# Attention and two feed-forward products on one core: v in six loads by SyncE, k asked for in mid-batch, six moves by GpSimd's queue

## The chip, the cores and the metric

The kernel runs on 1 core of one Trainium2 chip. The metric is the device time of one execution in microseconds (us); each kernel is timed in several runs and the median counts. One more execution of each kernel was recorded by the hardware profiler. All durations and waits below come from such a recording.

In the rows PE is TensorE (matmul), PEld its weight loads, DVE VectorE, ACT ScalarE, POOL GpSimd, SP SyncE. SP computes nothing here: it asks for transfers. A "q" behind an engine's name is its instruction queue: "SPq L281" is SP issuing the transfer of line 281.

## The reference

Attention over 4 batches of 12 heads (448 tokens, 64 wide) whose scores are mixed over the heads ahead of the softmax and again behind it; then two feed-forward products over the 1792 tokens.

```
scores = scale * np.matmul(q, k.transpose(0, 1, 3, 2))
scores = np.einsum('bhij,hg->bgij', scores, w_pre)
attn = softmax(scores)                       # exp(scores - max) / (sum + 1e-9)
attn = np.einsum('bhij,hg->bgij', attn, w_post)
x = np.matmul(attn, v)                       # -> 1792 x 768
x = ((x @ w1) * (x @ w2)) @ w3 @ w_out       # widths 1024, 1024, 768
out = leaky(x @ w_in) @ w_out2               # max(0.01 h, h), width 2048
```

## The kernel before

**Stages.** The attention fills the first 372 us of the span; what follows are the feed-forward products, in which TensorE is busy 99% of the time or more. The change touches the attention alone. The order of all instructions behind it is the same in both kernels, engine by engine.

**Tiling of the attention.** A batch's 448 rows of scores are cut into four chunks (120, 120, 120 and 88 rows). The 12 heads go in 6 pairs `p`. For each chunk and pair, `qk` (L242) makes the raw scores in PSUM, ACT or DVE copies them to a tile `s` (L254, L256), and `move` (L281) carries each head's rows by DMA from SBUF to SBUF into one of three row tiles `sr`, where rows of all heads stand in the partitions together, so that `premix` (L315) can mix the heads as one matmul. A chunk is 12 moves (the last head takes two pieces, so 13 transfers), 210 KB each for a full chunk. Then, for each group of two blocks of rows: `premix` (PE, pm), `tops` (DVE, mx, L325), `softmax` (ACT, e, L332), `weigh` (mostly POOL, e, L348: the division by the sum), `postmix` (PE, po, L369, and DVE transposes to `ap`, L384), and `av` (PE, px, L401), the product with v.

**The loop.** Groups are numbered through all batches, 23 a batch (6, 6, 6 and 5 a chunk). The main loop takes `k` = 0, 2, 4, ...; one turn is called a step, and `do(k // 2, ...)` counts them. A step runs `qk` for the groups ten ahead (LEAD), `tops` and `softmax` of groups k and k+1, `av` for two pairs of a finished chunk, `postmix` of groups k-2 and k-1, and `premix` of groups k+2 and k+3. The first `premix` of a chunk needs all its 13 moves landed. Chunk 2 of the first batch starts with group 12, mixed at the end of step k = 10.

**What sets the order.** The attention is written out by hand (`manual_schedule`): each engine takes its instructions in the order of the program text. `at(step, job, ...)` puts loads of q and k and their splits (`upper` on ACT, `lower` on DVE) at steps counted back from the step that needs them (`need`). Nearly all transfers are issued by SP, in order, on one queue. The program gives its SP and ACT transfers eight semaphores in turn, so that a transfer is issued only when the one that holds its semaphore from eight places earlier has landed.

**v and k.** `vs` holds v of one batch (six pairs, 256 KB each). Batch 0's v is one load of 1536 KB on ACT's queue at the end of step 0 (L551); those of batches 1 to 3 are three loads of 512 KB by SP, each behind the `av` of two pairs in the last chunk of the batch before. k of a batch is three loads of 448 KB (two pairs each), asked for four steps ahead of need. For batches 2 and 3 these are the very steps in which v is loaded too; call this stretch the seam between two batches. The row tiles of the chunks go on being filled through it.

**The start.** The ten groups' worth of `qk` that run ahead of the loop cover the first chunk and part of the second. The first chunk's moves are cut in two halves (105 KB each): first halves of even heads on ACT's queue, of odd heads on SP's; second halves of odd heads on SP's, and of the six even heads on ACT's queue, three at k = 7 and three at k = 9 of that first loop (L465).

Of the kernel before, what the change touches and what calls it, by code (L numbers as in the profile page):

```python
# [22 lines left out]
def attention_moe_kernel(ctx: ExitStack, tc, qt, kt, vt, w_pre, w_post, w1, w2, w3t, w_out, w_in2, w_out2, out):  # L23
# [7 lines left out]
    nc = tc.nc  # L31
    B, _, NPAIR, S = kt.shape
# [85 lines left out]
    def attention(seam):  # L118
        with ExitStack() as es, ExitStack() as left:
# [60 lines left out]
            NC = len(chunks)  # L180
            HN, PLAIN, KROOM, QROOM = NPAIR // 2, NC, 9, 7
            vs = late.tile([P, NPAIR, NJ, 2, D], F32, tag="vs", name="vs", bufs=1)
# [22 lines left out]
            def q_load(b, c, a):  # L205
                load("q", (b, c, a), qt[b, c][:, a * HN:(a + 1) * HN, :])
# [9 lines left out]
                lo_dve(lo, raws[key][1], hi)  # L216
                give(key[0], [raws.pop(key)])

            def v_load(b, p0, p1, queue=nc.sync):
                queue.dma_start(out=vs[:, p0:p1], in_=vt[b, p0:p1].rearrange("n p j e d -> p n j e d"))  # L220

            def qk(b, c, p, early=False):

# [214 lines left out]
            def slot(k):  # L438

                b, c, t, nt = where[k]  # L440
                return [(b, c, p) for p in range(NPAIR) if min(p, nt - 1) == t]
# [10 lines left out]
            for k in range(LEAD):  # L452
                for x in slot(k):
                    qk(*x, early=True)
                if k == 1:
                    turn(4)
                if k == 5:
                    constants()
                    for args in second[1::2]:
                        move(*args, nc.sync, 1)  # L460
                        if not queued and args[-1] > 4:
                            queued.append([q_load(*order[2], a) for a in range(2)])
                if k in (7, 9):
                    for args in second[(k - 7) * 3:][:6:2]:
                        move(*args, nc.scalar, 1)  # L465
            turn(6)

            jobs = {}
# [1 line left out]
            def at(step, job, *args):  # L470

                jobs.setdefault((max(step, 0), job), []).append(args)
# [17 lines left out]
            for i in range(3, len(order)):  # L490
                for a in range(2):
                    need = step_of(i, a * HN)
# [3 lines left out]
            for b in range(1, B):  # L496
                for g in range(HN):
                    need = step_of(b * NC, 2 * g)
                    at(need - 4, k_load, b, g)
                    parted("k", (b, g), need)  # L500

            premix(0)
# [3 lines left out]
            for k in range(0, NG + 2, 2):  # L506
                if k:
                    flush(queue=nc.scalar if k + LEAD > NG else nc.sync)
                while later:
                    stores.append(later.pop(0))  # L510
                now = [g for g in (k, k + 1) if g < NG]
                done = [g for g in (k - 2, k - 1) if g >= 0]
                fresh = [n for g in now for n in groups[g]]
                old = [n for g in done for n in groups[g]]
                before = ets.pop(k - 2, None)
                ahead = [x for g in now if g + LEAD < NG for x in slot(g + LEAD)]
                for x in ahead:
                    qk(*x)
                for job in (k_load, q_load):
                    do(k // 2, job)  # L520
                if fresh:
                    tops(fresh)
                    sm, ets[k] = softmax(fresh)
                evict()
                do(k // 2, lower)
                drain = not ahead
                for _ in range(min(4 if len(todo) > NPAIR else 2, len(todo)) if now else len(todo)):
                    b, c, p = todo.pop(0)
                    av(b, c, p)
                    if c == NC - 1 and b < B - 1 and p % 2:  # L530
                        v_load(b + 1, p - 1, p + 1)
                turns = []
                if drain:
                    if old:
                        turns = postmix(old, before, now=False)
                        turn_out(turns.pop(0))
                    if k > LAST:
                        next(seam, None)
                    if now:
                        weigh(fresh, sm, ets[k], True)  # L540
                    while turns:
                        turn_out(turns.pop(0))
                else:
                    weigh(fresh, sm, ets[k], False)
                while lows:
                    lows.pop(0)()
                if old and not drain:
                    postmix(old, before)
                do(k // 2, upper)
                if not k:  # L550
                    v_load(0, 0, NPAIR, nc.scalar)  # L551
                for g in done:
                    b, c, t, nt = where[g]
                    if t == nt - 1 and (b, c) != order[-1]:
                        todo += [(b, c, p) for p in range(NPAIR)]
                if not k:
                    turn(8)
                for g in (k + 2, k + 3):
                    if g < NG:
                        premix(g)  # L560
                if k == LAST:
                    left.close()
                    next(seam)
# [569 lines left out]
```

## Time and profile before

| | us |
|---|---|
| median of 3 runs (lowest, highest) | 1229.01 (1226.84, 1230.17) |
| the profiled execution | 1230.43 |
| its span, first to last instruction | 1228.6 |
| TensorE busy in the span | 1204.7 |
| VectorE busy | 886.0 |
| ScalarE busy | 551.7 |
| GpSimd busy | 209.8 |

The table is read from its third row: the span is what the rows below are about, and the profiled execution lies 1.4 us above the median. TensorE is busy nearly all the time, but a matmul counts as busy at half clock too, so idle time of PE and its clock have to be read together, stretch by stretch. The rows by which this is done stand in a section of their own below.

### The profile page before, as it was taken

How to read it: one execution, taken by the hardware profiler on the slowest of the kernel's cores; microseconds unless marked ns; L12 is line 12 of the kernel's file. 1: busy time of each engine (PE TensorE's matmuls, PEld its weight loads, DVE VectorE, ACT ScalarE, POOL GpSimd, SP SyncE). 2: the span in 40 equal slices, each digit the busy share in tenths (PEclk: the TensorE clock that was granted, in tenths of full speed). 3: DMA queues.
4: the chain of work that ended last, by engine and by line, in shares of the span. 5: the costliest groups of instructions: out<-in, count | busy, mean ns of one | idle time of the engine just before them, and what ended most of it. 6: DMA issues, size and time to landing. Idle time of an engine off the chain costs nothing.

```text
span 1228.6 us, 22434 instructions
## 1 busy us (share of the span) xinstructions
PE 1204.7 (98%) x8782; PEld 988.4 (80%) x8782; DVE 886.0 (72%) x1525; ACT 551.7 (45%) x1118; POOL 209.8 (17%) x163
## 2 busy tenths in 40 slices
PE   8899899999999999999999999999999999999998
PEld 5255455455468989998999999999999999999998
DVE  5587877888789998636795968557776758376672
ACT  2587776776664554322454433352333333323120
POOL 4467757656410000000000000000000000000000
PEclk9799999999999999999999999999999999999999
DMA  6756866856777666569764646053332221212012
GB/s 187 233 155 185 215 192 174 236 180 179 219 264 251 229 205 191 187 223 337 260 213 158 212 126 219 26 204 120 99 107 90 65 70 52 66 38 71 26 52 90
DMA packets 135906, 196.81 MB, mean 160 GB/s; under 512 B 26392, under 2 KB 115064, under 8 KB 135800
## 3 DMA queue, kind: packets, MB, share of 16 engines
q1 hardware_dynamic: 131040, 191.14, 48.7%
q10 hardware_dynamic: 4760, 4.24, 1.2%
q8 instruction: 69, 1.13, 0.4%
q14 instruction: 37, 0.30, 0.1%
HBM read 114.57 MB, written 42.07 MB: 127 GB/s over the span
## 4 chain that ended last, share of the span: by engine, by line
PE 82%; DVE 6%; DMA 5%; ACT 4%; issue 1%; POOL 0%; ACTq 0%; SPq 0%; DVEq 0%; POOLq 0%
PE pm L596 29%; PE po L610 19%; PE pp L907 17%; PE pw L668 6%; DMA sr<-s 5%; PE px L401 5%; DVE ap L384 4%; PE po L369 3%; ACT e L332 3%; PE pm L315 2%; PE pq L242 2%; DVE mx L325 1%; ACT s L256 1%; PE turn L302 1%; POOL e L348 0%
## 5 line engine op out<-in xcount | busy, mean ns | idle before, releaser
L596 PE MATMUL pm<-x,ws 128*128 128x384 f32 (+1 forms) x1152 | 233.9, 364 | 0.0
L596 PEld LDWEIGHTS pm<-x,ws 128*128 128x128 f32 x1152 | 208.7, 188 | 24.5 <-issue 0.6
L348 POOL TENSOR_SCALAR e<-e,sm 128x448 f32<-128x448 f32 x128 | 184.7, 1455 | 148.4 <-DVE sm L342 128.6
L332 ACT ACTIVATE e<-pm,mx 128x448 f32<-128x448 f32 x180 | 111.7, 632 | 82.1 <-DVE mx L325 75.6
L384 DVE STREAM_TRANSPOSE ap<-po 128x512 f32<-128x512 f32 (+3 forms) x216 | 115.9, 595 | 28.3 <-PE po L369 27.6
L907 PE MATMUL pp<-t,w 128*128 128x448 f32 x576 | 124.5, 368 | 0.0
L610 PE MATMUL po<-ws,g 128*128 128x384 f32 x672 | 117.2, 334 | 0.0
L610 PE MATMUL po<-wo,g 128*128 128x384 f32 x672 | 117.1, 334 | 0.0
L907 PEld LDWEIGHTS pp<-t,w 128*128 128x128 f32 x576 | 108.1, 188 | 10.9
L610 PEld LDWEIGHTS po<-wo,g 128*128 128x128 f32 x672 | 116.6, 188 | 0.2
L610 PEld LDWEIGHTS po<-ws,g 128*128 128x128 f32 x672 | 116.6, 188 | 0.0
L325 DVE TENSOR_REDUCE mx<-pm 128x1 f32<-128x448 f32 x180 | 98.9, 605 | 13.8 <-PE pm L315 13.8
L100 ACT ACTIVATE wc<-wr 128x768 f32<-128x768 f32 (+1 forms) x72 | 61.6, 859 | 88.6 <-DMA wr<-in_moe_w_dram 29.4
L315 PE MATMUL pm<-sr,kpre 64*64 64x448 f32 x720 | 87.2, 563 | 12.4 <-DMA sr<-s 12.4
L401 PEld LDWEIGHTS px<-ap,vs 96*64 96x64 f32 (+1 forms) x1536 | 77.7, 136 | 22.8 <-ACT e L332 17.5
L907 PE MATMUL pp<-b,w 128*128 128x448 f32 x432 | 95.6, 368 | 0.0
L256 ACT ACTIVATE s<-pq 120x448 f32<-120x448 f32 (+1 forms) x179 | 83.5, 559 | 23.7 <-DMA sr<-s 11.1
L617 DVE TENSOR_TENSOR acc<-po,acc 128x384 f32<-128x384 f32 x84 | 45.6, 556 | 65.7 <-PE po L610 65.5
L369 PE MATMUL po<-e,kpost 64*32 64x512 f32 (+1 forms) x1472 | 90.8, 598 | 0.8 <-POOL e L348 0.7
L401 PE MATMUL px<-ap,vs 96*64 96x120 f32 (+3 forms) x1536 | 87.6, 266 | 3.6 <-ACT e L332 1.8
L907 PEld LDWEIGHTS pp<-b,w 128*128 128x128 f32 x432 | 81.0, 188 | 8.0
L315 PEld LDWEIGHTS pm<-sr,kpre 64*64 64x64 f32 x720 | 26.8, 134 | 72.6 <-issue 26.2
(105 smaller groups left out, 1601.9 us busy)
## 6 DMA issues: line engine op xcount, KB each, us to landing
sr<-s SPq DMA_DIRECT2D x121, 210.0 KB
wr<-in_moe_w_out_dram SPq DMA_DIRECT2D x24, 768.0 KB
wr<-in_moe_w_dram SPq DMA_DIRECT2D x16, 768.0 KB
wr<-in_moe_w_in_dram SPq DMA_DIRECT2D x16, 768.0 KB
wr<-in_moe_w_dram SPq DMA_DIRECT2D x16, 512.0 KB
sr<-s SPq DMA_DIRECT2D x44, 157.5 KB
kept_w<-wc SPq DMA_DIRECT2D x16, 384.0 KB
sa<-kept_w SPq DMA_DIRECT2D x16, 384.0 KB
```

The source lines that it names most:

```text
L256: nc.scalar.activation(out=t[:m, e, :], in_=pq[e][:m], func=ACTF.Copy)
L315: nc.tensor.matmul(pms[ns[s % len(ns)]][half:half + Q], kpre[rows], sr[rows, 2 * t + g, :], start=True, stop=True,)
L325: nc.vector.tensor_reduce(out=mxs[n], in_=pms[n], axis=AX.X, op=ALU.max, negate=True)
L332: ends["act"] = nc.scalar.activation(out=e[:, i], in_=pms.pop(n), func=ACTF.Exp, bias=mxs.pop(n), scale=1.0, accum_out=sm[:, i:i + 1])
L348: ends["dve" if eng is nc.vector else "pool"] = eng.tensor_scalar(out=e[:, i], in0=e[:, i], scalar1=rc[:, i:i + 1], scalar2=None, op0=ALU.mult
L369: nc.tensor.matmul(po[g][32 * r:32 * (r + 1), :m], kpost[rows, x], e[rows, :m, JS[r]:JS[r] + P], start=True, stop=True,)
L384: ends["dve"] = nc.vector.transpose(out=dst, in_=po[g][:, i0:i1])
L401: nc.tensor.matmul(px[e * D:(e + 1) * D, r, :nw].rearrange("p (n i) -> p n i", i=HQ), vs[rows, p, jc, e, :], ap[rows, x, :ns, jc, h * HQ:( ...
L596: nc.tensor.matmul(dst, wt[:, a, kk, :], x[kk][:, c, c0:c0 + w], start=(i == 0), stop=(i == len(steps) - 1))
L610: nc.tensor.matmul(po, g[m][:, a, t * P:(t + 1) * P], wts[m][:, c, cs], start=(m == 0 and j == 0), stop=(m == FQ - 1 and j == 2),)
L668: nc.tensor.matmul(pw, wt[:, x, kk, :], wos[kk][y][:, cs], start=(kk == 0 and j == 0), stop=(kk == KF - 1 and j == 2),)
L907: nc.tensor.matmul(dst, w[:, i, a, kk, :], b[:, kk, c, :], start=(kk == 0 and j == 0), stop=(kk == KH - 1 and j == 2),)
```

## The change

Three edits, all in the attention.

```
-            def v_load(b, p0, p1, queue=nc.sync):
-                queue.dma_start(out=vs[:, p0:p1], in_=vt[b, p0:p1].rearrange("n p j e d -> p n j e d"))
+            def v_load(b, p):
+                nc.sync.dma_start(out=vs[:, p], in_=vt[b, p])
...
                 if k in (7, 9):
                     for args in second[(k - 7) * 3:][:6:2]:
-                        move(*args, nc.scalar, 1)
+                        move(*args, nc.gpsimd, 1)
...
                     need = step_of(b * NC, 2 * g)
-                    at(need - 4, k_load, b, g)
+                    at(need - 10 + g if b > 1 else need - 3, k_load, b, g)
...
                     av(b, c, p)
-                    if c == NC - 1 and b < B - 1 and p % 2:
-                        v_load(b + 1, p - 1, p + 1)
+                    if c == NC - 1 and b < B - 1:
+                        v_load(b + 1, p)
...
                 if not k:
-                    v_load(0, 0, NPAIR, nc.scalar)
+                    for p in range(NPAIR):
+                        v_load(0, p)
```

With `need` = 6, 7, 8 for batch 1, 18, 19, 20 for batch 2 and 29, 30, 31 for batch 3, the k loads go from steps 2, 3, 4 to 3, 4, 5 (batch 1), from 14, 15, 16 to 8, 10, 12 (batch 2) and from 25, 26, 27 to 19, 21, 23 (batch 3).

On ACT at the start of the program (`sr` is the row tile of the first chunk, `s` a copy of raw scores, `e` the exponentials, `vs` is v):

```order
 L281 DMA sr_108<-s 10x6x448 x2
-L256 ACTIVATE s<-pq 120x448 x2
-L281 DMA sr_108<-s 10x6x448 x3
-L256 ACTIVATE s<-pq 120x448 x2
-L281 DMA sr_108<-s 10x6x448 x3
-L332 ACTIVATE e,sm<-pm,mx 128x448 x4
-L256 ACTIVATE s<-pq 120x448 x4
-L220 DMA vs<-in_v_dram 128x6x512
+L256 ACTIVATE s<-pq 120x448 x4
+L332 ACTIVATE e,sm<-pm,mx 128x448 x4
+L256 ACTIVATE s<-pq 120x448 x4
```

Six moves and the one large load leave ACT's queue; its copies of scores stand together now.

On SP at the same place (`sr_106` is the second chunk's row tile, `sr_107` the third's):

```order
 L281 DMA sr_106<-s 10x12x448 x11
 L281 DMA sr_106<-s 5x12x448 x2
-L200 DMA q<-in_q_dram 128x360
-L281 DMA sr_107<-s 10x12x448 x4
-L200 DMA k<-in_k_dram 128x896
+L220 DMA vs<-in_v_dram 128x512 x6
+L200 DMA q<-in_q_dram 128x360
+L281 DMA sr_107<-s 10x12x448 x4
```

The six loads of v stand between the second chunk's last moves and the third chunk's first; one k load moves one step down. The six moves that ACT loses stand on POOL between its clearing of tiles (L154) and the first division (L348).

On SP at the seam between the first and the second batch (`scr` is a store of finished rows; `sr_108` is batch 1's third chunk, `sr_106` its fourth):

```order
-L220 DMA vs<-in_v_dram 128x2x512
+L220 DMA vs<-in_v_dram 128x512 x2
 L296 DMA scr_57<-y 768x1x120 x2
-L200 DMA k<-in_k_dram 128x896
 L200 DMA q<-in_q_dram 128x360
 L281 DMA sr_108<-s 10x12x448 x4
-L220 DMA vs<-in_v_dram 128x2x512
-L200 DMA k<-in_k_dram 128x896
+L220 DMA vs<-in_v_dram 128x512 x2
 L200 DMA q<-in_q_dram 128x360
 L281 DMA sr_108<-s 10x12x448
 L281 DMA sr_108<-s 5x12x448 x2
```

Two k loads of 448 KB no longer stand ahead of the last moves of `sr_108`; v takes as many bytes in twice as many transfers.

## Rows read from the trace of the kernel before

**Rows 1.** The page: the span, and the engines' busy time.

```profile
span 1228.6 us, 22434 instructions
PE 1204.7 (98%) x8782; PEld 988.4 (80%) x8782; DVE 886.0 (72%) x1525; ACT 551.7 (45%) x1118; POOL 209.8 (17%) x163
```

**Rows 2.** Chain of work that ended last: start us, us, what; transfers in it.

```profile
35.88 10.82 DMA sr<-s
...
141.76 11.49 DMA sr<-s
```

**Rows 3.** Timeline, PE, start: start us, us, what, xcount [idle before <-releaser].

```profile
27.16 1.20 PE L315 MATMUL pm<-sr,kpre 64*64 64x448 f32 x8 [1.81 <-DMA sr<-s]
...
31.32 3.34 PE L242 MATMUL pq<-k,q 64*120 64x448 f32 x6 [2.02 <-ACT s L256]
...
46.90 4.54 PE L315 MATMUL pm<-sr,kpre 64*64 64x448 f32 x16 [3.43 <-DMA sr<-s]
...
57.66 1.73 PE L315 MATMUL pm<-sr,kpre 64*64 64x448 f32 x16
...
71.86 1.74 PE L315 MATMUL pm<-sr,kpre 64*64 64x448 f32 x16
```

**Rows 4.** Timeline, PE: a premix of batch 1's second chunk; first and second seam.

```profile
127.98 1.74 PE L315 MATMUL pm<-sr,kpre 64*64 64x448 f32 x16
...
148.44 0.98 PE L315 MATMUL pm<-sr,kpre 64*64 64x448 f32 x8
153.45 2.67 PE L315 MATMUL pm<-sr,kpre 64*64 64x448 f32 x8 [4.03 <-DMA sr<-s]
156.05 3.58 PE L242 MATMUL pq<-k,q 64*90 64x448 f32 x18
...
241.15 0.97 PE L315 MATMUL pm<-sr,kpre 64*64 64x448 f32 x4 [0.39 <-DMA sr<-s]
242.71 1.72 PE L315 MATMUL pm<-sr,kpre 64*64 64x448 f32 x12 [0.58 <-DMA sr<-s]
244.36 2.07 PE L242 MATMUL pq<-k,q 64*90 64x448 f32 x18
```

**Rows 5.** Stretches: length; busy PE, PEld, DVE, ACT, POOL; PEclk; DMA share; GB/s.

```profile
24.00:28.00 4.00, 2.19 (x20) 0.90 (x19) 1.96 (x5) 1.05 (x4) 3.21 (x3) 1.00 0.32 94
28.00:34.00 6.00, 3.98 (x12) 1.82 (x8) 1.16 (x2) 3.28 (x10) 1.11 (x1) 0.64 0.69 191
...
47.00:57.00 10.00, 10.00 (x48) 3.02 (x56) 3.51 (x8) 4.75 (x12) 3.83 (x4) 0.50 0.81 240
57.00:69.00 12.00, 12.00 (x145) 5.26 (x131) 10.05 (x20) 7.83 (x22) 5.87 (x5) 1.00 0.74 210
69.00:72.00 3.00, 3.00 (x56) 1.44 (x56) 2.65 (x7) 3.00 (x11) 1.43 (x1) 1.00 0.30 99
...
119.00:122.00 3.00, 3.00 (x62) 1.70 (x60) 1.77 (x7) 3.00 (x10) 1.35 (x1) 1.00 0.48 150
...
130.00:154.00 24.00, 19.34 (x270) 10.18 (x268) 18.07 (x41) 17.24 (x49) 16.72 (x15) 0.97 0.92 236
```

**Rows 6.** SP's waits in 18:48: engine line, what ended them, us, times, longest.

```profile
SPq L281 <- DMA vs<-in_v_dram: 6.5, 1, 6.5
SPq L281 <- DMA sr<-s: 3.0, 3, 2.0
```

**Rows 7.** Timeline of POOL, and instructions of L152: ns least, median, most.

```profile
10.44 0.15 POOL L154 MEMSET spare<- 128x65 f32 x1
24.79 4.33 POOL L348 TENSOR_SCALAR e<-e,sm 128x448 f32<-128x448 f32 x3 [14.20 <-ACT s L256]
...
L152 POOL MEMSET sr<- x2: 4577/4578/4578, 1.2 to 5.7; 128x5376 f32 x2
```

**Rows 8.** Instructions that write sr, 0:60: ACT's issues; and k's size.

```profile
L281 ACTq DMA_DIRECT2D sr<-s x12: 778/779/1427, 8.0 to 20.8; - x12
...
k<-in_k_dram SPq DMA_DIRECT2D x12, 448.0 KB
```

## The prediction

> **What bounds the kernel now.** I read the page first: a span of 1228.6 us with PE busy for 1204.7 [rows 1]. So behind the attention there is little to win, and none of it is touched. In the attention the chain of work that ended last is the next view: it goes through long transfers, of which two of about 11 us from issue to landing are moves of score rows, at 35.88 and 141.76 us [rows 2]. The reader is to see there that PE is not short of work but of rows. The timeline of PE then says what each costs. At the start PE waits three times for such rows or for a copy that is held up by them: 1.81, 2.02 and 3.43 us, 7.26 in all [rows 3]. At the first seam it waits 4.03 us, at the second 0.39 and 0.58 [rows 4]. And it pays again behind the long waits, by its clock: in 47:57 the granted clock was 0.50 [rows 5], the lower of the two levels (1.2 and 2.4 GHz), and the same 16 matmuls take 4.54 us where they later take 1.73 [rows 3]. The third wait of the start and the one of the first seam, the two of 3.4 us and over, were followed by that; those of the second seam were not.
>
> The views of the transfers say why. Around the first seam (130:154) the DMA engines were busy for 0.92 of the time at 236 GB/s [rows 5]: there the transfers are the bound. At the start they are the bound in part only: 0.69 at 191 GB/s with moves alone in 28:34, but 0.32 just ahead of it [rows 5], while SP sat 3.0 us behind moves and 6.5 us behind the one large load of v that held its semaphore [rows 6].
>
> **The change part by part: the seams.** Two k loads leave the queue ahead of the moves for which PE waits at 153.45. At 448 KB each [rows 8], 0.917 MB by the 236 GB/s of that stretch [rows 5], that is 3.9 us of transfer. The wait is 4.03. Part of a load runs on DMA engines that the moves leave idle (0.69 is the share with moves alone), and v is now two issues where it was one, so I take 3.1, with 3.9 as the upper end; a rest of 0.9 is as short as the waits of the second seam, which brought no lower clock. The half clock then goes too: 2.67 us for 8 premix matmuls against about 0.87 (half of 1.74), and 3.58 for 18 matmuls of `qk` against 2.07 [rows 3, 4], that is 1.8 + 1.5 = 3.3. First seam: 6.4, between 3.1 (the lower clock stays) and 7.2. Second seam: the waits of 0.39 + 0.58 go, 1.0, between 0 and 1.0. At the third seam no k is loaded, so only the splitting of v is left: nothing in the trace waits for three more short issues, 0.
>
> **Where k goes to.** Its new steps lie at about 90, 105 and 117 us for batch 2, beside moves and stores. The place to watch is 117: there k stands right ahead of the last moves of batch 1's second chunk, which premix needs at 127.98 [rows 4]. In 119:122 the share was 0.48 against the 0.69 of a full queue of moves [rows 5], so about 0.9 us of the load's 1.9 (0.459 MB at 236 GB/s) fits at once; the rest delays moves that are due some microseconds later. I put 0.3 us on it, between 0 and a wait like that of the first seam, 4.0 + 3.3 = 7.3.
>
> **The start.** Six moves leave ACT's queue at 0.78 us of issue each [rows 8]. ACT itself waited for VectorE's maxima there, so that alone gives nothing. What counts is when the third chunk's rows are there, for its first premix at 71.86 [rows 3]. Three terms:
> - Slack before. The share fell from 0.74 in 57:69 to 0.30 in 69:72 [rows 5], so the backlog ended near 69. Its last piece was a k load (1.9 us), so the rows were there near 67.1 and had 4.8 us to spare.
> - One k load less stands ahead of them (batch 1's go one step down): 1.9 us.
> - The gap in 24:28 closes, since six transfers no longer take turns with SP's for semaphores and SP's issues come up to 3 us earlier: (1 - 0.32 / 0.69) x 4 = 2.1 us.
>
> That is 8.8 us at most before the transfers bind. Against it stands v, now in SP's queue between the second and the third chunk's moves instead of beside the second's. Its bytes are the same and lie ahead of 71.86 in both kernels, so I charge 1.0, between 0 and 2.0, for what no longer overlaps with moves. The wait of 6.5 us behind the one load goes, and the premix at 46.90 comes some 5 us sooner; but PE will then run ahead and stand before the third chunk in one long wait, with the half clock behind it. Such a stretch cost (57.66 - 46.90) - (71.86 - 57.66) / 2 = 3.7 us [rows 3]; as part of it lies under the wait itself, I take 2.3. Start: 8.8 - 1.0 - 2.3 = 5.5. The lower end is 0 (the rows come no sooner). The upper end is what PE lost there, 7.3 of waits and 3.7 of clock, 11.0.
>
> **Moves on POOL.** No row shows a transfer issued by POOL. It is free from 10.59 and first needed at 24.79 [rows 7]: 14.2 us for six, so up to 2.37 us each cost nothing. The lower bound is ACT's 0.78 [rows 8], the upper the longest thing that POOL does, clearing a row tile, 4.58 [rows 7]. I take a value near ACT's, as the same 105 KB are described, and so 0.
>
> The Trainium skill speaks against this part: "SBUF — State Buffer", section "SBUF: two separate sides", warns that descriptors of a POOL transfer cannot be written while VectorE runs an operation that uses both shared ports; its next section gives 620 ns alone and some 3100 ns beside such operations. By 3.1 us each POOL would be free at 29.2, 4.4 late, and the sum would be 8.2 instead of 12.6, 1220.8 us. Whether VectorE's copies from PSUM at this place count among them no run here shows.
>
> **Sum.** 5.5 + 6.4 + 1.0 - 0.3 = 12.6 us off the profiled span of 1228.6, which becomes 1216.0. That execution took 1230.43, 1.4 above the median of 1229.01; off the median it is **1216.4**. Nothing behind the attention changes its order, and PE is full there, so I let the whole gain reach the end.
>
> **The rivals.**
> - The start gives nothing, because transfers bound it anyway and v in front of the third chunk takes what the gap gave: 1229.0 - 7.1 = 1221.9. For it: 0.81 of DMA share in 47:57 [rows 5]. Against it: the 4.8 us of slack.
> - All waits go, and the clock stays up: 11.0 + 7.2 + 1.0 = 19.2, 1209.8. For it: only the transfers held PE up there. Against it: the bytes ahead of 71.86 are the same but for one k.
> - k at 117 us makes a wait of its own ahead of 128, with half clock behind: 12.6 - 7.0 = 5.6, 1223.4.
> - The change relieves nothing: moves wait as long behind v in pieces as behind v and k, about 1229. Against it: 3.9 us of transfers less in a stretch that is 0.92 busy.
> - Slower: POOL's issues take 4.58 us each. Then POOL is free at 10.6 + 27.5 = 38.1, 13.3 late, and the first divisions and all behind them come that much later. The waits at 27.16 and 46.90 absorb 1.81 + 3.43 of it; the long idle brings one more stretch of half clock, 3.7; the seams still give 7.1: 1229.0 + 13.3 - 5.2 + 3.7 - 7.1 = 1233.7. It begins to cost above 2.37 us each, turns the sign at 3.8 and counts as slower from 4.4.
>
> **How the numbers follow.** Forecast 0.47; start gives nothing 0.20; all waits go 0.14; a new wait for k 0.08; no relief 0.06; POOL slow 0.05. (The page's 3.1 us would land among the second group, for 0.04 of its 0.20.) A measurement of this kernel tells about 0.3%, 3.7 us, from no change: faster is below 1225.3, slower above 1232.7. Faster: 0.47 + 0.20 + 0.14 and most of the new wait, 0.06, is 0.87; slower 0.05; same 0.08. The range goes from a little under the second rival, 1208.5, to 1226.0, the smallest seam gain (3.1) with nothing else; it leaves out no relief, slow POOL and a few strays.
>
> **What would show it.** Right: PE's wait of 4.03 at the first seam under 1 us and the granted clock at 1.00 through it; a premix of the second chunk near 42 instead of 46.90, and one of the third chunk near 65 instead of 71.86 that waits for moves; POOL's first division still near 25; no wait of PE near 115 to 130. Wrong: a wait of over 3 us left at the seam, a third chunk's premix still 71 us in, divisions on POOL after 29, or a PE idle stretch at a chunk's first premix in mid-batch.

## The result, and the profile after

The changed kernel takes 1218.59 us (median of 6 runs, 1214.08 to 1221.53) against 1228.62 us (6 runs) for the kernel before: a ratio of 0.9918, 95% interval 0.9897 to 0.9938, so 10.0 us less. The forecast was 1216.4. In the profiled execution the span is 1216.7 us against 1228.6, 11.9 less. Two profiles are two executions: that of before took 1230.43 us, 1.8 above its median here, that of after 1218.51, which is 0.1 from its own. Differences of 1 to 2 us between two profiles are therefore not laid to an edit below unless the trace shows what they wait for.

The page of after, answering to [rows 1], with the queue that GpSimd now uses (packets, MB, share of 16 engines):

```profile
span 1216.7 us, 22474 instructions
PE 1198.3 (98%) x8782; PEld 986.5 (81%) x8782; DVE 885.7 (73%) x1525; ACT 550.5 (45%) x1118; POOL 213.0 (18%) x169
...
q0 software_dynamic: 288, 0.65, 0.2%
```

Two transfers of its chain of work that ended last (start us, us, what), answering to [rows 2]:

```profile
42.33 6.67 DMA sr<-s
...
138.10 6.36 DMA sr<-s
```

The two moves of about 11 us are gone from the chain, but moves are still in it at the same two places, the start and the first seam. The timeline of PE at both, and at the second seam (columns as in [rows 3]), answering to [rows 3, 4]:

```profile
21.08 1.85 PE L315 MATMUL pm<-sr,kpre 64*64 64x448 f32 x16 [3.03 <-DMA sr<-s]
...
40.18 0.97 PE L315 MATMUL pm<-sr,kpre 64*64 64x448 f32 x4
41.47 1.72 PE L315 MATMUL pm<-sr,kpre 64*64 64x448 f32 x12 [0.32 <-DMA sr<-s]
...
46.78 0.98 PE L315 MATMUL pm<-sr,kpre 64*64 64x448 f32 x8
49.70 2.19 PE L315 MATMUL pm<-sr,kpre 64*64 64x448 f32 x8 [1.94 <-ACT s L256]
...
58.09 1.73 PE L315 MATMUL pm<-sr,kpre 64*64 64x448 f32 x16
...
65.19 1.74 PE L315 MATMUL pm<-sr,kpre 64*64 64x448 f32 x16
...
121.31 1.74 PE L315 MATMUL pm<-sr,kpre 64*64 64x448 f32 x16
...
141.77 0.98 PE L315 MATMUL pm<-sr,kpre 64*64 64x448 f32 x8
144.46 1.94 PE L315 MATMUL pm<-sr,kpre 64*64 64x448 f32 x8 [1.71 <-DMA sr<-s]
146.33 3.33 PE L242 MATMUL pq<-k,q 64*90 64x448 f32 x18
...
153.35 1.74 PE L315 MATMUL pm<-sr,kpre 64*64 64x448 f32 x16
...
230.16 1.73 PE L315 MATMUL pm<-sr,kpre 64*64 64x448 f32 x16
```

The last of these lines is the premix of the second seam, at 241.15 in before; it waits for nothing now. Read against [rows 3, 4], the same premixes give PE's lead over the kernel before, place by place:

| premix | before | after | lead |
|---|---|---|---|
| second chunk, first | 46.90 | 40.18 | 6.7 |
| second chunk, second | 57.66 | 46.78 | 10.9 |
| third chunk, first | 71.86 | 65.19 | 6.7 |
| batch 1's second chunk | 127.98 | 121.31 | 6.7 |
| first seam, first half | 148.44 | 141.77 | 6.7 |
| `qk` behind it | 156.05 | 146.33 | 9.7 |
| premix of the next step | 163.34 | 153.35 | 10.0 |

Behind the second seam the lead is 11.6 (the postmix of one step at 248.23 and 236.66), and the attention ends 11.95 earlier. So the start gave 6.7, the first seam 3.3, the second 1.6, and the third 0.4, where a wait of 0.41 us at 320.42 of before is gone. The second row of the table holds the surprise: 10.9 us had been won by 46.78, and 4.2 were given back within one step, 46.78 to 58.09, which takes 11.3 us where the next takes 7.1. PE waits there for a copy of raw scores by ACT (49.70), and ACT for a move (ACT's instructions, columns as in [rows 3]):

```profile
49.11 0.98 ACT L256 ACTIVATE s<-pq 120x448 f32<-120x448 f32 x2 [2.53 <-DMA sr<-s]
```

Stretches of [rows 5] in after, and the one behind the wait at the first seam (columns as there):

```profile
24.00:28.00 4.00, 4.00 (x36) 2.38 (x32) 1.55 (x5) 2.19 (x7) 2.07 (x2) 1.00 0.46 139
...
47.00:57.00 10.00, 8.06 (x72) 3.41 (x72) 5.20 (x11) 6.21 (x16) 6.73 (x6) 0.83 0.77 231
...
123.00:147.00 24.00, 21.67 (x284) 11.18 (x282) 19.60 (x45) 17.97 (x51) 17.06 (x15) 0.97 0.84 217
...
146.00:149.00 3.00, 3.00 (x16) 2.00 (x16) 2.58 (x7) 2.43 (x7) 0.03 (x1) 0.50 0.61 203
```

The gap ahead of 28 has closed in part, from 0.32 to 0.46 of DMA share, and the seam, taken 7 us earlier because PE reaches it 6.7 us earlier, has gone from 0.92 at 236 GB/s to 0.84 at 217. Behind 146 the granted clock is 0.50, and `qk` takes 3.33 us for 18 matmuls, little less than the 3.58 of [rows 4]. SP's waits in 18:48, answering to [rows 6]:

```profile
SPq L281 <- DMA sr<-s: 1.6, 2, 1.3
...
SPq L281 <- DMA vs<-in_v_dram: 0.2, 1, 0.2
```

The timeline of GpSimd, answering to [rows 7]:

```profile
10.54 2.39 POOL L281 DMA_DIRECT2D sr<-s  x4
13.47 1.10 POOL L281 DMA_DIRECT2D sr<-s  x2 [0.54 <-ACT s L256]
25.93 4.33 POOL L348 TENSOR_SCALAR e<-e,sm 128x448 f32<-128x448 f32 x3 [11.36 <-ACT s L256]
```

And the instructions that write `sr` in 8:22, answering to [rows 8] (ns least, median, most):

```profile
L281 ACTq DMA_DIRECT2D sr<-s x6: 778/792/1717, 8.0 to 14.1; - x6
L281 POOL DMA_DIRECT2D sr<-s x6: 553/553/746, 10.5 to 14.0; - x6
```

SP's 6.5 us behind the one load of v are 0.2 now, and GpSimd has issued its six moves by 14.6, 11 us ahead of its first division.

### The profile page after: what moved, and what is told of

Same layout as the page of the kernel before. It is cut to its first block, busy times and chain, and to the rows that moved or that the text cites. A ratio compares the mean times of both kernels' runs of the same rounds, so it can differ in the third digit from the quotient of the medians.

```text
span 1216.7 us, 22474 instructions
## 1 busy us (share of the span) xinstructions
PE 1198.3 (98%) x8782; PEld 986.5 (81%) x8782; DVE 885.7 (73%) x1525; ACT 550.5 (45%) x1118; POOL 213.0 (18%) x169
## 3 DMA queue, kind: packets, MB, share of 16 engines
q10 hardware_dynamic: 3556, 2.02, 0.6%
## 4 chain that ended last, share of the span: by engine, by line
PE 84%; DVE 8%; ACT 4%; DMA 3%; issue 1%; ACTq 0%; POOL 0%; SPq 0%; DVEq 0%; POOLq 0%
PE pm L597 29%; PE po L611 19%; PE pp L908 17%; DVE ap L384 6%; PE px L401 6%; PE pw L669 6%; PE po L369 4%; ACT e L332 3%; DMA sr<-s 3%; PE pq L242 2%; PE pm L315 2%; DVE mx L325 1%; PE turn L302 1%; ACT s L256 0%; DVE e L348 0%
## 5 line engine op out<-in xcount | busy, mean ns | idle before, releaser
L348 POOL TENSOR_SCALAR e<-e,sm 128x448 f32<-128x448 f32 x128 | 184.5, 1454 | 132.6 <-DVE sm L342 116.0
L908 PEld LDWEIGHTS pp<-t,w 128*128 128x128 f32 x576 | 108.1, 188 | 10.9
L315 PE MATMUL pm<-sr,kpre 64*64 64x448 f32 x720 | 84.0, 554 | 7.0 <-DMA sr<-s 5.1
L72 ACT ACTIVATE ws<-wc 128x768 fp32r<-128x768 f32 (+1 forms) x64 | 49.7, 788 | 69.6 <-PE po L611 45.2
```

The source lines that it names most:

```text
L315: nc.tensor.matmul(pms[ns[s % len(ns)]][half:half + Q], kpre[rows], sr[rows, 2 * t + g, :], start=True, stop=True,)
L348: ends["dve" if eng is nc.vector else "pool"] = eng.tensor_scalar(out=e[:, i], in0=e[:, i], scalar1=rc[:, i:i + 1], scalar2=None, op0=ALU.mult
L908: nc.tensor.matmul(dst, w[:, i, a, kk, :], b[:, kk, c, :], start=(kk == 0 and j == 0), stop=(kk == KH - 1 and j == 2),)
```

## The experiments

First each part alone on the kernel before, and the change without the moves on GpSimd's queue; these four ran on one chip (before: 1227.04).

**The moves alone.**

```
-                        move(*args, nc.scalar, 1)
+                        move(*args, nc.gpsimd, 1)
```

> The kernel before with the third edit alone: the six second halves of the first chunk's moves go by POOL's queue. Theory A (the start's 6.7 us come from v, not from POOL's queue; POOL's moves compete with the first halves): the first premix comes about 2 us later than 18.84, the wait of about 6.5 us of SP behind the one load of v stays, premix of the third chunk stays within 2 us of 71.86, the seams are as before; 1227 to 1230 us. Rival B (the six moves off ACT's queue and its semaphores bring the start's gain): premix of the third chunk near 65 to 67, some 5 us faster, 1222 to 1224.

Measured: 1227.84 us, ratio 1.0002 (0.9992 to 1.0012). Theory A: no gain and no loss by itself. The first premix came at 21.11, not 18.84, as in after.

**The k loads alone.**

```
-                    at(need - 4, k_load, b, g)
+                    at(need - 10 + g if b > 1 else need - 3, k_load, b, g)
```

> The kernel before with the second edit alone: k of batches 2 and 3 asked for in mid-batch, of batch 1 one step later; v is loaded as before (one load on ACT's queue, then three by SP). Theory A (k is what filled the queue at the seams): PE's wait at the first seam falls from 4.03 to 1 to 2 us and that step is 3 to 4 us shorter, the second seam 1 to 1.6 us shorter, the start within 1.5 us of before; 1222.5 to 1225 us. Rival B (the splitting of v at the seams brings it): the first seam keeps a wait of 3 us or more, total within 1.5 us of before.

Measured: 1225.35 us, ratio 0.9989 (0.9980 to 0.9999), between the two theories. In its profile the start gains 2.5 us and the second seam 1.6, as in after. But the first seam gains 1.3 only: two k loads less ahead of the moves leave most of the wait there (timeline of PE):

```profile
146.23 0.98 PE L315 MATMUL pm<-sr,kpre 64*64 64x448 f32 x8
150.03 2.50 PE L315 MATMUL pm<-sr,kpre 64*64 64x448 f32 x8 [2.82 <-ACT e L332]
```

(The releaser named is ACT. The matmul also reads the moved rows, and by the landings in the trace (a transfer has landed with the last event on its semaphore) a move of these rows lands at 149.83, 0.2 us before PE goes on.) So 3.1 us for the two k loads was too much.

**Batch 0's v alone, in six loads by SP.**

```
-                    v_load(0, 0, NPAIR, nc.scalar)
+                    for p in range(NPAIR):
+                        v_load(0, p, p + 1)
```

> The kernel before with the first edit at the start alone: batch 0's v in six loads by SP at step 0; later v in three loads as before, k and the six moves as before. Theory A (the one load of v held SP's last moves of the second chunk): SP's wait of 6.5 us behind v goes, premix of the second chunk comes near 42 instead of 46.90, ACT then waits some 2 us for its copies of the third chunk behind v; premix of the third chunk 4 to 6 us earlier than 71.86; 1222.5 to 1225. Rival B (v in front of the third chunk's moves costs what it gave): premix of the third chunk within 1.5 us of 71.86, 1227 to 1230.

Measured: 1225.72 us, ratio 0.9992 (0.9976 to 1.0008), so no gain beyond the noise. The profiled execution took 1230.32, 4.6 above the median. It shows the same pattern as after: 11.0 us won at the second chunk's second premix (46.66 against 57.66), 7.0 of them given back by the third chunk's first (67.81 against 71.86), where after gives back 4.2. Who waited there, among ACT's instructions (start us, us, what [idle before <-releaser]):

```profile
49.85 0.98 ACT L256 ACTIVATE s<-pq 120x448 f32<-120x448 f32 x2 [3.43 <-DMA sr<-s]
...
57.69 0.97 ACT L256 ACTIVATE s<-pq 90x448 f32<-90x448 f32 x2 [3.38 <-DMA sr<-s]
```

ACT copies raw scores into a tile `s`; the tile is free when the move that reads it has landed, and that move stands behind the six loads of v. In the kernel before, the copies between 40 and 72 us wait 0.71 us at most for a move.

**v and k without the moves.** The changed kernel with this line undone:

```
-                        move(*args, nc.gpsimd, 1)
+                        move(*args, nc.scalar, 1)
```

> The changed kernel with the third edit undone: the six second halves are back on ACT's queue. Theory A (POOL's queue delays the first premix by 2.2 us and gives little back): first premix near 19 instead of 21.08; the third chunk's premix within 2 us of 65.19 either way; 1215 to 1219. Rival B (POOL's queue is a needed part of the start's gain): premix of the third chunk 3 us later or more, 1220 to 1222.

Measured: 1220.19 us, ratio 0.9940 (0.9917 to 0.9963); 6.9 us of the gain, and the interval overlaps that of the whole change. The third chunk's premix comes at 65.52, as theory A has it, but the median lies in rival B's range, so how much the moves add on top of v and k is not shown. At the start the profiles add up, 2.5 and 4.1 alone, 6.3 together, though two executions of one kernel can differ by 2 us there, as the changed kernel run again shows below. At the first seam they do not, and the profile shows why it is a poor place to compare single executions (timeline of PE, then the stretch behind it, columns as in [rows 5]):

```profile
143.18 0.98 PE L315 MATMUL pm<-sr,kpre 64*64 64x448 f32 x8
145.89 3.08 PE L315 MATMUL pm<-sr,kpre 64*64 64x448 f32 x8 [1.72 <-DMA sr<-s]
```

```profile
147.00:153.00 6.00, 6.00 (x30) 3.10 (x30) 3.40 (x7) 3.72 (x9) 1.47 (x1) 0.50 0.69 189
```

The wait is that of after, 1.72 against 1.71. But behind it the clock stayed at half for six microseconds and more, where in after it was back after about three. One wait, two prices. It also shows a wait where the prediction looked for one on account of k in mid-batch: 0.52 us at 123.12 for moves, and a step 1.1 us longer. That k makes it is not shown by a run of its own. After shows none there.

The next four change the changed kernel itself (before on their chip: 1227.03).

**v of batch 0 later**, two loads a step:

```
-                if not k:
-                    for p in range(NPAIR):
+                if k in (2, 4, 6):
+                    for p in (k - 2, k - 1):
                         v_load(0, p)
```

> The changed kernel, but batch 0's v is loaded two pairs at a time in steps k = 2, 4 and 6 and no longer in six at step 0. Theory A (the six loads of v hold up the third chunk's first moves, these hold tiles s, and ACT's next copy waits for one; PE gave 4.2 us of its lead back there): PE's wait of 1.94 us at 49.70 and the half clock behind it go, the third chunk's first premix comes near 61.5 instead of 65.19, and the median falls by 3 to 4 us, to about 1215. Rival B (the bytes ahead of that premix bind, in whatever order): the wait goes from 49.70 but comes back as a wait for moves ahead of the third chunk's premix, which stays within 1 us of 65.2, and the median stays within 1.5 us of 1218.6.

Measured: 1220.55 us, ratio 0.9941 (0.9923 to 0.9960). Theory A had the wait right and the gain wrong. The wait at 49.70 is gone, the third chunk's first premix comes at 61.78, and by the postmix of the next step (71.38 against 71.70) the lead over after is down to 0.3 us. The second half of rival B is wrong too, since no move is waited for. The timelines of ACT and of PE:

```profile
65.66 0.95 ACT L72 ACTIVATE k<-k 128x896 fp32r<-128x896 f32 x1 [3.65 <-DMA k<-in_k_dram]
```

```profile
61.78 2.67 PE L315 MATMUL pm<-sr,kpre 64*64 64x448 f32 x16
...
67.27 0.46 PE L242 MATMUL pq<-k,q 64*120 64x448 f32 x1 [1.15 <-ACT e L332]
```

v now stood ahead of batch 1's k. ACT splits k into two parts, waited 3.65 us for it, and the exponentials of the next groups are queued behind that split.

**v later at the seams**: from the third pair on, the loads of the next batch's v come one step later, behind the last moves of the chunk.

```
                     if c == NC - 1 and b < B - 1:
-                        v_load(b + 1, p)
+                        if p < 2:
+                            v_load(b + 1, p)
+                        else:
+                            vnext.append((b + 1, p))
...
                 evict()
+                while vnext:
+                    v_load(*vnext.pop(0))
```

> The changed kernel, but at each seam the loads of v from the third pair on are asked for one step later, behind the moves for which PE waits. Theory A (v ahead of the last moves is what is left of the first seam's wait): the wait of 1.71 us goes under 0.4 and the half clock behind it (1.07 us in 8 premix matmuls, 1.26 in 18 of qk) goes with it: 3.3 to 4.0 us at the first seam, median about 1215. Rival B (moves queue behind moves there, v or not): the wait stays above 1.2 us and the median within 1.5 us of 1218.6. Rival C (k of batch 2 has already gone and the stretch is bound by bytes of stores, moves and v together): the wait goes from the first step of the seam and comes back at the next, with no gain.

Measured: 1214.62 us (1213.58 to 1215.43), ratio 0.9892 (0.9871 to 0.9913). Theory A: the wait is gone and the clock stays up (timeline of PE, then the stretch).

```profile
140.50 1.73 PE L315 MATMUL pm<-sr,kpre 64*64 64x448 f32 x16
142.17 1.99 PE L242 MATMUL pq<-k,q 64*90 64x448 f32 x13
```

```profile
140.00:149.00 9.00, 8.71 (x118) 4.38 (x106) 7.40 (x15) 8.06 (x23) 6.89 (x6) 1.00 0.89 248
```

The transfers are as busy as ever there, 0.89 at 248 GB/s. What changed is which of them come first.

**GpSimd's moves in reverse order**, so that it starts to issue at 13.6 instead of 10.5:

```
-                    for args in second[(k - 7) * 3:][:6:2]:
+                    for args in second[(9 - k) * 3:][:6:2][::-1]:
```

> The changed kernel, but the six moves that GpSimd issues come in the reverse order, three pairs later first, so that GpSimd begins to issue only near 13.7 instead of 10.5 us. Theory A (premix of the first chunk comes 2.2 us later than before, at 21.08 with a wait of 3.03, because second halves go out early and take DMA time from the first halves that this premix needs): the premix starts near 19, its wait falls under 1.5 us, and the second half of the first chunk is mixed no later than 27. Rival B (the first halves are late for another reason, SP's own order or the loads of q and k): the premix stays within 0.5 us of 21.1. Either way the median moves by less than 2 us, since the next chunk's moves bind behind it.

Measured: 1219.07 us, ratio 0.9929 (0.9902 to 0.9955), and the first premix at 21.04 with a wait of 3.64. That is rival B's outcome, but it doesn't acquit the second halves: at 13.6 they still go out ahead of the last first halves, so the edit did not move them far enough to tell. More telling is the first premix over all profiles: 18.4 to 19.4 in the four with these moves on ACT's queue, 19.9 to 21.9 in the ten with them on GpSimd's. The seam of this execution tells more than its start (timeline of PE): PE reached it at 141.77 as in after, to the hundredth, and waited 0.33 us instead of 1.71.

```profile
141.77 1.98 PE L315 MATMUL pm<-sr,kpre 64*64 64x448 f32 x12
144.08 0.97 PE L315 MATMUL pm<-sr,kpre 64*64 64x448 f32 x4 [0.33 <-DMA sr<-s]
```

**All three** edits of these last runs together.

> The edits of the last three runs together. If each removes the cost that I give it (4.2 us of give-back at 49.70, 3.3 at the first seam, up to 2 at the first premix), the attention ends 7 to 9 us earlier than in the changed kernel and the median is near 1211. If the bytes bind in either place, it is the sum of what the single runs gave, or less.

Measured: 1216.00 us, ratio 0.9907 (0.9888 to 0.9925): the seam's gain, nothing from the start. That is the second of the outcomes named, the sum of the single runs or less.

The next three ran on one chip (before: 1227.65).

**v later at the seams, k back in them.** The kernel with v later at the seams, and

```
-                    at(need - 10 + g if b > 1 else need - 3, k_load, b, g)
+                    at(need - 4 if b > 1 else need - 3, k_load, b, g)
```

> The kernel of e6_seam_v (v from the third pair on one step later at each seam) with the k loads of batches 2 and 3 put back to four steps ahead of need, so into the seams. Theory A (both k and v stand ahead of the moves for which PE waits, and each is worth its bytes): with 0.9 MB of k back, PE waits 2 to 3.5 us at the first seam and the half clock follows, so the first seam loses 3 to 6 us against e6_seam_v; waits of 0.4 to 1.5 us come back at the second; median 1218 to 1221. Rival B (v behind the moves was the whole cure, and asking for k early was not needed at the first seam): the wait stays under 0.5 us and the median within 1.5 us of e6_seam_v.

Measured: 1220.59 us, ratio 0.9947 (0.9932 to 0.9963). Theory A, with less wait than it asked for but the loss that it named: from the first seam's first premix to the next step's 11.9 us instead of 8.4, and 0.86 us of wait at the second seam, there for v itself (product with v, 227.29).

```profile
141.60 0.98 PE L315 MATMUL pm<-sr,kpre 64*64 64x448 f32 x8
143.83 0.97 PE L315 MATMUL pm<-sr,kpre 64*64 64x448 f32 x4 [1.25 <-DMA sr<-s]
145.29 1.21 PE L315 MATMUL pm<-sr,kpre 64*64 64x448 f32 x4 [0.50 <-DMA sr<-s]
```

So at the first seam k and v are each enough to make a wait, and a stretch of half clock in this execution and in after; the wait goes only when neither k nor the loads of v from the third pair on stand ahead of these moves.

**Batch 0's v in pairs** at steps k = 0, 2 and 4, on the kernel with v later at the seams:

```
-                if not k:
-                    for p in range(NPAIR):
+                if k in (0, 2, 4):
+                    for p in (k, k + 1):
                         v_load(0, p)
```

> The kernel of e6_seam_v with batch 0's v in pairs at steps k = 0, 2 and 4: between the six at step 0 of the changed kernel and the two a step at k = 2, 4, 6 of e5_late_v0. Theory A (what e5_late_v0 gained at 49.70 it lost again because v then stood ahead of batch 1's k, for which ACT waited 3.65 us with the exponentials queued behind): here no v stands behind the first of those k loads, ACT's wait for k falls under 1.5 us, and the third chunk's second step ends 1 to 2.5 us earlier than in the changed kernel; median 1212 to 1214. Rival B (the bytes of v, k, q and moves that are due by 72 us bind in any order): postmix of step 5 stays within 0.7 us of e6_seam_v, median within 1.2 us of it.

Measured: 1217.71 us, ratio 0.9921 (0.9906 to 0.9936). Theory A falls: ACT's wait for k was still 2.32 us, and the one for q ahead of it 5.23, where the kernel with all six loads at step 0 waits 2.03 and 2.40. The postmix that the expectation counts as that of step 5 (it stands in the step k = 12, and starts at 71.70 in after) came 3.5 us later than there. ACT, then PE:

```profile
60.21 0.50 ACT L72 ACTIVATE q<-q 128x360 fp32r<-128x360 f32 x1 [5.23 <-DMA q<-in_q_dram]
```

```profile
62.22 3.47 PE L401 MATMUL px<-ap,vs 96*64 96x120 f32 x32 [4.54 <-ACT e L332]
```

**The changed kernel again**, not a line different.

> The changed kernel itself once more, beside the other two on one chip, with another profile. Theory A (its first seam is decided anew in every execution: the same instructions at the same times wait between 0.3 and 3 us there, with no, 3.4 or 6.8 us of half clock behind, and that is most of the spread of 7 us between its runs): the second profile has the same times up to 140 us within 0.5 us, or a start shifted by up to 1.5 us, and another wait at the seam. Rival B (the wait belongs to the order of the queue and repeats): 1.71 within 0.3 us and 3.4 us of half clock.

Measured: 1219.96 us (1214.55 to 1222.79), ratio 0.9931 (0.9909 to 0.9953). Theory A, and more than it said, in an execution of 1214.55, the fastest of its six: the start came 2.1 us earlier than in the first profile, and the first seam waited 0.77 and 0.35 us with the clock at 1.00 all through (timeline of PE, then the stretch). The step of the seam takes 9.7 us here and 11.6 in the first profile.

```profile
139.67 0.98 PE L315 MATMUL pm<-sr,kpre 64*64 64x448 f32 x8
141.42 0.97 PE L315 MATMUL pm<-sr,kpre 64*64 64x448 f32 x4 [0.77 <-DMA sr<-s]
142.75 0.97 PE L315 MATMUL pm<-sr,kpre 64*64 64x448 f32 x4 [0.35 <-DMA sr<-s]
```

```profile
139.00:149.00 10.00, 8.88 (x114) 4.20 (x98) 7.12 (x14) 8.72 (x23) 7.10 (x6) 1.00 0.84 208
```

**ACT's splits behind its copies.** The kernel with v later at the seams, in which batch 1's k and first q are split by ACT one half step later (`upper_late` does what `upper` does; before on this chip: 1227.89):

```
-                at(need - 2, upper, kind, key)
+                if key[0] == 1 and (kind == "k" or key[1] == order[PLAIN][1]):
+                    at(need - 1, upper_late, kind, key)
+                else:
+                    at(need - 2, upper, kind, key)
...
+                do(k // 2, upper_late)
                 do(k // 2, lower)
```

> The kernel of e6_seam_v, in which ACT's splits of batch 1's first q and its k stand behind the copies of scores of the next step instead of ahead of its exponentials. Theory A (the lead of the start is lost because ACT waits 2.0 to 2.4 us each for q and k with the exponentials queued behind these splits): the exponentials of these steps no longer come behind a wait for q or k, the steps from 53 to 70 us are 2 to 4 us shorter in sum, and the median falls to 1211 to 1213. Rival B (all that is due by 72 us is bound by the rate of the transfers): the same time is lost as PE's wait for moves, or for the splits one step on; postmix of step 5 within 0.8 us of 70.4 (start shifts of one execution aside), median within 1.2 us of 1214.6.

Measured: 1224.46 us, ratio 0.9970 (0.9960 to 0.9981): some 10 us worse than without the edit, and neither theory. ACT no longer waited for q or k ahead of its exponentials, and up to the postmix before that one (61.53 against 61.40) the start was level. But VectorE makes the second part of each split from the first, in its own order, and stood there with the maxima behind it (timeline of DVE); PE's next steps stretched and the half clock came at 91.5.

```profile
63.44 0.53 DVE L75 TENSOR_TENSOR q<-q 128x360 fp32r<-128x360 f32 x1 [3.23 <-ACT q L72]
...
75.21 1.09 DVE L75 TENSOR_TENSOR k<-k 128x896 fp32r<-128x896 f32 x1 [4.54 <-ACT k L72]
```

**The first seam over all profiles.** Worked out from the timelines of PE as shown above: from the first premix of the seam to that of the next step, and the wait in it for moved rows (in four of them the view names ACT or a load of q as the releaser, and a move of these rows lands at most 0.5 us before PE goes on). "v(0)" is batch 0's v, "again" the second profile of the changed kernel. Each profile is one execution: that of v(0) alone took 4.6 us more than its runs' median, reverse order 3.2 and again 5.4 us less.

| ahead of the last moves | profiles | step, us | PE's wait for rows |
|---|---|---|---|
| k, v in loads of two pairs | before, moves alone, v(0) alone | 14.9, 14.3, 17.0 | 4.03, 4.17, 4.37 |
| v in loads of two pairs | k alone | 13.6 | 2.82 |
| v in single loads | after, again, reverse order | 11.6, 9.7, 9.0 | 1.71, 1.12, 0.33 |
| v in single loads | v and k, later v(0) | 13.4, 13.2 | 1.72, 2.96 |
| k, v of the first two pairs | v later, k back | 11.9 | 1.75 |
| v of the first two pairs | v later; all three; v(0) in pairs; splits late | 8.4 in each | none |

## Why the prediction was right, and where its steps were off

**The sum.** 12.6 us were forecast, 11.9 came off the span and 10.0 off the median. Three of its terms were right in sign and near in size; the one that carried half of it was twice too large, and smaller terms made up for it. That the sum came so close is in part luck. Of the signs named, the second chunk's premix (near 42; 40.18 and 41.47), the third's (near 65; 65.19, but without a wait for moves), GpSimd's first division (near 25; 25.93) and the absence of a wait at 115 to 130 came; the one at the first seam, under 1 us at full clock, did not.

**First seam: 6.4 forecast, 3.3 found (5.2 in the second profile; 3.5 on average over the five with v in single loads and k early), the step that failed.** What a seam without wait is worth was read rightly: 14.9 us in before, 8.4 where nothing is waited for, so 6.5. The error was to give all of it to k. I divided k's bytes by the rate of the stretch and took the 3.1 us off the wait of 4.03, as if nothing else stood there. The run of k alone took 1.2 us off the wait; with v in single loads as well, 1.71 us were left. The runs of v later and of k back show the rest: v, whose bytes had stayed ahead of the same moves, is worth as much again, and only both edits together end the wait. The rows of SP's order in the part on the change show two loads of v, with one of q behind them, in front of the last three moves of `sr_108`, and two more ahead of the four moves before; I had read them as a matter of issues, two where there was one, and not of their bytes, 0.5 MB a pair of loads. The second half of the term, the clock, followed from the first: a wait of 1.71 us was still followed by half clock, where I had counted on a rest of 0.9. The prediction's rows held a warning: I wrote that only the two waits of 3.4 us and over were followed by half clock, but 28:34, with the wait of 2.02 us, has a granted clock of 0.64, and six matmuls of `qk` take 3.34 us there [rows 3, 5].

**Start: 5.5 forecast, 6.7 found (8.8 in the second profile).** The rows came about as reckoned: 8.8 less 1.0 for v is 7.8, and by the landings in the trace the third chunk's last move lands at 63.74, 8.1 us ahead of 71.86 (at 67.60 in before, where I had read off 67.1). The charge for a long wait with half clock, 2.3, became 4.2, given back from a lead of 10.9 at 46.78; of these the rows show 1.94 of wait and 2.1 of half clock (8 matmuls of premix in 2.19 us instead of about 0.87, 8 of `qk` in 2.57 instead of 1.74). The place was wrong: PE did not stand at the third chunk's first premix for moves. It stood two premixes earlier, for ACT's copies, whose tiles were held by moves behind v. The rows of before had shown such an indirect wait, of 2.02 us at 31.32, and I had counted it without asking what it means for v: ACT waited for a move there too (ACT's instructions of before).

```profile
30.72 0.54 ACT L256 ACTIVATE s<-pq 120x448 f32<-120x448 f32 x1 [5.67 <-DMA sr<-s]
```

The rival in which the start gives nothing fell. But the thought behind it has something: the runs with v at two other places moved the wait to k (3.65) and to q (5.23), the run with late splits to VectorE (4.54), and that same postmix, of k = 12, came at 71.4 to 74.0 in them, where the changed kernel has it at 69.6 and 71.7. Whether the bytes due by 72 us set the limit, or a better order exists, stays open; I found none.

**Second and third seam: 1.0 and 0 forecast, 1.6 and 0.4 found.** The waits of [rows 4] went; 0.64 us for the product with v at 236.91 of before, which I had not counted, went with them.

**k in mid-batch: 0.3 forecast.** Nothing in after at 115 to 130, and 0.52 us of wait with 1.1 us of loss at the same place in v and k without the moves. The place was right, and the margin there is small.

**GpSimd's queue: 0 forecast, 0 found.** Its issues take 553 ns in the median, under the lower bound of 0.78 us; its first division starts at 25.93, not 24.79, because the first premix comes later. That premix is what I missed: 21.08 with a wait of 3.03 us, where before had it earlier and with a shorter wait, a fourth one at the start beside the three that I counted (timeline of PE in before):

```profile
18.84 1.89 PE L315 MATMUL pm<-sr,kpre 64*64 64x448 f32 x16 [1.71 <-DMA sr<-s]
```

In before, ACT issued its second halves between 15.87 and 21.6, when all first halves were issued and about half of them there; GpSimd issues them in 10.5 to 14.6, beside the first halves. By the landings in the traces three of these first halves, issued at the same times to 0.02 us (near 13.2, 13.8 and 14.1), take 3.7, 4.1 and 4.2 us to land in before and 6.4 each in after. The Trainium skill ("DMA: Bandwidth & Descriptors", section "Issuing engines are not separate DMA queues") says that transfers of all issuing engines interleave on the same 16 DMA engines, so that a second queue saves issue time alone. The trace agrees with that, by these three moves and by the first premix, which is 2.2 us later; the wait of 1.81 us for these second halves at 27.16 went in return, and the run of the moves alone made the balance zero. It did so on the kernel before; on top of v and k the balance is not shown.

The Trainium skill's warning that I had weighed ("SBUF — State Buffer", section "SBUF: two separate sides") did not bear on the copies here. GpSimd's first four issues took 2.39 us while VectorE copied from PSUM for 2.42 of 2.50 us, so these copies did not hold them up; what an operation that uses both shared ports would do, no run here shows:

```profile
10.50:13.00 2.50, 2.50 (x16) 1.20 (x14) 2.42 (x5) 0.76 (x2) 2.43 (x6) 1.00 0.61 159
```

**What stays open.** In medians batch 0's v alone and k alone give 1.3 and 1.7 us, both together 6.9. The profiles explain a part (at the start they add up). The rest may be v in single loads at the seams, which only the combined kernels have: the table's second row differs in it from the third and fourth, by 13.6 us in one profile against a mean of 11.4 over five, which range from 9.0 to 13.4. It was not tried alone.

**A version that is likely faster than both.** With v later at the seams the kernel takes 1214.6 us, about 4 us under the changed kernel; the intervals, 0.9871 to 0.9913 against 0.9897 to 0.9938 and 0.9909 to 0.9953 in its two measurements, overlap a little with the first and just with the second. Its four runs lie within 1.9 us, the twelve of the changed kernel within 8.7. In its own profile PE still waits 1.40 us at the second seam, ahead of a product with v (223.19).

## What to carry to other kernels

When a wait sits behind a shared queue, list all that stands ahead of the awaited transfer, with its bytes, before giving the wait to one of them: taking one away uncovers the next, and here only both ended it. Ask also what the delayed transfers hold, for a buffer that is released late stalls an engine that never reads the loaded data. And where a stretch differs between executions, compare kernels there by several profiles or by the spread of the runs, not by one.

## What the runs showed of the hardware

- One wait has more than one price. Waits of 1.71 and 1.72 us at the same place were followed by about three and by over six microseconds at a granted clock of 0.50, and waits of 0.77 and 0.35 by none. The steps took 11.6, 13.4 and 9.7 us, where the step without a wait takes 8.4.
- The same instructions of a seam wait differently from one execution to the next. Two programs that differ only in the order of six moves at the start reached the seam at the same time to 0.01 us (141.77, in after and in the run with the reverse order), and waited 1.71 and 0.33 us for the same rows; the changed kernel itself waited 1.71 and 1.12 us in its two profiles. The three of its twelve runs under 1215 us have a mean granted clock of 0.999 or 1.000, the other nine 0.994 to 0.998. Much of the spread is likely this seam, but that is not shown: where its wait is gone, eight runs of two kernels lie within 4 us and six of a third within 4.5, but the four runs with k back, which wait there, lie within 3.2.
- GpSimd issues a move of 105 KB in 553 ns in the median, where ACT takes 779 to 792.
